# The last two heads' rows moved into the spare rows of the output projection's chunks, with a new written order for the last stages

## The chip, the cores and the metric

The kernel runs on one core of a Trainium2 chip. The metric is device microseconds of one execution, as the median of several. TensorE is called PE, VectorE DVE, ScalarE ACT, GpSimd POOL, and the engine that issues all DMAs here is SyncE, SP.

## The reference

One input x of 2048 rows and 640 columns goes through a linear attention with 32 heads of 20 and through a feed-forward layer of width 1728; a sigmoid gate g per row mixes the two.

```python
qkv = x @ wqkv                                    # 32 heads of 20
pq, pk = q @ w_phi, k @ w_phi                     # per head
phi = concat(softmax(p), softmax(-p))             # 40 features per head, of q and of k
kv, z = phi_k^T @ v, sum(phi_k)
o = (phi_q @ kv) / (phi_q @ z + 1e-6)
a = o @ wo
b = silu(x @ w1) @ w2
out = g * a + (1 - g) * b
```

## The kernel before

Everything is float32. Where accuracy matters PE multiplies in float32r, and each operand is split into a high and a low part, hi and lo; a product is then three passes, hi by hi, hi by lo, lo by hi. Splitting takes a copy on ACT (hi) and a subtraction on DVE or POOL (lo).

The rows of x are worked on as 16 tiles of 128, 8 blocks of 256 or 4 of 512. The first stages compute keys and values of all tiles and sum kv and z. Then the feed-forward layer runs, with the written orders HEAD and O1 to O10, in block products with fewer multiplications; its gated output goes to DRAM, as fb_d. The stage TAIL finishes the feed-forward layer, builds the query weights WQ (w_phi folded into wqkv, from loads of wqT) and does the queries of the last four tiles. The last stage, FIN, does the queries of the other twelve tiles, and for every block u the product with kv and the projection with wo.

An order is a string of names, and each name is a few instructions. The context manager `inorder` (L236) binds the instructions of PE, DVE, ACT and POOL to the order in which they are written, each engine for itself; SP isn't bound by it and is placed by the framework's scheduler. Before, each stage has its own `inorder`, so that instructions of two neighbouring stages can be interleaved.

The names of TAIL that matter here: fl is a load of 120 rows of wqT, fm the PE work that folds w_phi into them (L347), fs its split into WQ; hm and hp are the rest of the hidden tiles (L686) and their SiLU and split; im, ia and ig are output products, their addition and the gated store; km and kp make the weights kvw and kvwr from kv; ol and os load and split wo.

The names of FIN, with a query tile b of 0 to 11, a block u of 0 to 7, and p for a projection step:

- q0p and so on: the query projection, 30 matmuls (L596). q0m: maximum and minimum per head (L580, L581). q0s0, q0s1: the two differences (L587). q0e: the exp (L1335). q0S: sums (L1339). q0z: the product with z on POOL (L1352). q0Z: its sums (L1355). q0P, q0i, q0k: five small DVE steps (L1366 to L1382). q0M: scaling on POOL (L1388).
- t and f: t03 is PE's transposes of the features of block 0, group 3 (L1611), f03 the copy out of PSUM. Five groups hold six heads each, 120 features on either side; group 5 holds the last two heads, 80 features.
- n: the matmuls with kvw (L1727). The two sides of a group go to rows 0 to 63 and 64 to 127 of one bank. Each side has three heads, thus 60 rows; the four rows up to 64 are zero and unused.
- h and l: the split of n's result into oT, hi and lo (L1738, L1741 and L1747), for chunks 0 and 1, 2 and 3, and 4. A chunk is 128 rows of oT; there are five.
- w: the projection (L1780). Step p = 0, 1, 2 takes two blocks, 512 columns; steps 3 and 4 one block each, 256 columns. The digits after p are a part m0 of the output's five; in steps 3 and 4 the parts 0 and 2 do two at once. a and b are its two halves. d adds the feed-forward's part y, loaded from fb_d (L1772), and stores to out (L1791, L1792).
- x: x5l loads x columns for later queries (L321), x5s splits them.

The last two heads' 40 rows fit into no chunk. Before, kvwr is the 80 by 40 matrix three times side by side, so that n of group 5 gives 120 rows, three copies of the 40; `stk`, a small table of signs loaded from cst, turns them into hi, lo and hi (L1742, L1749), in the tile oR. wo's 40 rows are stacked in the same way in WOR (name R; L1286, L1287). One matmul of oR with WOR is then all three passes at once, the sixteenth term of a projection:

```python
TERMS = [(c, ho, hw) for ho, hw in PASSES for c in range(NG)] + [(NG, 0, 0)]
```

Of the kernel before, what the change touches and what calls it, by code (L numbers as in the profile page):

```python
# [8 lines left out]
F32 = mybir.dt.float32  # L9
F32R = mybir.dt.float32r  # L10
# [6 lines left out]
P = 128  # L17
S = 2048
D = 640
# [56 lines left out]
fl1 W fl5 fm1 fl2 fs1 fm0 ol1 fl3 hm012 fm2 fs0 fl4 fm3 fs2 fs3 wa hm013 hp012 fm5 fm4 fs4 hm113 fs5  # L76
km hp013 hm112 kp os1 qp12 hp113 q012 hp112 ol0 q112 qe12 wb qs12 im0 qn12 ia0 qN12 im1 qc12 qp13 ig0
q013 ia1 ol4 qP12 qi12 im2 q113 ol3 qe13 ia2 qw12 qs13 qm12 qc13 ol2 im3 qn13 ia3 ig1 qN13 qP13 os2
qp14 os0 qi13 q014 ig2 xl1 im4 q114 qw13 ig3 xl0 ia4 qm13 im5 os3 qe14 qs14 qn14 xs0 xs1 qc14 qp15
qN14 qP14 q015 ig4 xl2 ia5 im6 qi14 tm0 qw14 q115 tm1 qm14 os4 to0 qe15 qn15 ig5 qs15 ia6 ig6 qN15  # L80
to1 im7 ia7 qc15 im8 ia8 qP15 tm2 im9 qi15 ia9 xs2 tm3 ig7 qw15 qm15 ig8 ig9 to2 to3
# [62 lines left out]
t04 R t05 q0p q0m n000 n001 f04 f05 n010 h00 x5l n011 q0s0 h01 l00 l01 n020 n021 t10 h02 t11 f10 f11  # L144
l02 q0s1 t12 q1p t13 f12 x6l t14 q0e f13 q0z t15 q0S f14 q1m f15 q1s0 q1s1 q0Z n100 n101 h10 n110
n111 n120 x3s n121 h11 h12 q1e x4s x7l x8l x5s l10 l11 l12 x9l q0P q0i q1z q0k q0M q1S w00a w00b q1Z
w01a w01b q1P q1i d00 q1k q1M q2p q2m q2s0 q2s1 q2e d01 w02a w02b d02 q2z x6s x10l x7s x11l x8s x12l
t20 f20 t21 f21 t22 q3p q2S f22 t23 f23 q2Z t24 f24 t25 f25 q3m q3s0 q3s1 q3e q2P q2i q2k q3z q3S
n200 q2M n201 h20 n210 n211 h21 n220 n221 h22 w03a l20 q3Z w03b x9s q3P q3i l21 q3k l22 d03 q4p w04a
w04b q4m q4s0 q4s1 q4e q3M q5p q4z d04 q4S x13l x10s x11s x14l x15l t30 f30 q4Z t31 q4P f31 t32 f32  # L150
t33 q4i f33 t34 q5m f34 t35 f35 n300 q5s0 n301 q5s1 h30 n310 n311 h31 n320 n321 h32 q5e q4k q5z l30
q4M l31 l32 q5S w10a q5Z q5P w10b q5i q6p w11a w11b q5k q5M d10 q6m q6s0 d11 w12a w12b q6s1 q6e d12
q6z q6S x12s x16l x13s x14s x17l q7p t40 f40 t41 f41 t42 f42 t43 f43 q6Z t44 f44 q7m t45 f45 q7s0
q7s1 q7e q6P q6i q6k q7z q7S n400 n401 q6M h40 n410 n411 h41 n420 n421 h42 l40 q7Z q7P q7i q7k q7M
w13a w13b l41 l42 x15s d13 q8p w14a x16s x17s q8m q8s0 q8s1 q8e t50 f50 w14b d14 q8S q8z q9p q8Z t51
f51 t52 f52 t53 t54 f53 f54 t55 q9m q9s0 f55 q9s1 n500 n501 n510 h50 n511 h51 n520 n521 h52 q9e q8P
q8i q8k q9z l50 l51 q8M l52 q9S w20a w20b q9Z q9P q9i d20 q9k q9M q10p w21a w21b w22a q10m q10s0
q10s1 q10e d21 q10S w22b d22 q10z t60 f60 t61 f61 t62 q11p f62 t63 f63 q10Z t64 f64 t65 q11m f65
q11s0 q11s1 q11e q10P q10i q10k q11z n600 n601 h60 n610 n611 h61 q10M q11S n620 l60 q11Z n621 h62
q11P l61 q11i q11k l62 w23a q11M w23b d23 w24a w24b w30a d24 w30b d30 t70 f70 t71 f71 t72 f72 t73 f73  # L160
t74 f74 t75 f75 n700 n701 h70 n710 n711 h71 n720 n721 h72 l70 l71 l72 w32a w32b d32 w34a w34b d34
w40a w40b w42a d40 w42b d42 w44a w44b d44
# [8 lines left out]
def mix_kernel(ctx: ExitStack, tc: tile.TileContext, xT, wqT, wkc, wkr, wv, bd, bdc, cst, wo, w1, w1r, w2, out):  # L171
# [31 lines left out]
    def single(name):  # L203

        k = turns["single"] = turns.get("single", -1) + 1
        return ps.tile([P, 512], F32, tag=f"single{k % 4}", name=name, bufs=1)
# [29 lines left out]
    def inorder(*engines):  # L236
# [4 lines left out]
        prev = {}  # L241
# [16 lines left out]
    stk = cp.tile([P, 4], F32, name="stk")  # L258
# [16 lines left out]
    g_d = dp.tile([NT, P], F32, name="g_d")  # L275

# [49 lines left out]
    def xb_split(p, lo_eng="pool"):  # L326
        u, c = XP[p]
        r = xb.pop(p)
        t = slot(f"xb_{u}_{c}")
        split(t[:, 0, : r.shape[1]], t[:, 1, : r.shape[1]], r, lo_eng)  # L330
        if c == 0:
            X["t", u] = []
        X["t", u].extend(t[:, :, k * 256 : (k + 1) * 256] for k in range(r.shape[1] // 256))
# [233 lines left out]
    nc.sync.dma_start(stk, cst)  # L567
# [317 lines left out]
    with inorder(PE, ACT, DVE, POOL):  # L885
# [61 lines left out]
        with inorder(PE):  # L947
# [18 lines left out]
            nc.scalar.activation(warms, stk[:, :1], AF.Silu)  # L966
# [317 lines left out]
    def stack(dst, src, hi, col, n=GW):  # L1284

        nc.scalar.activation(hi, src, AF.Copy, scale=stk[:n, col : col + 1])  # L1286
        nc.vector.scalar_tensor_tensor(  # L1287
            dst, src, stk[:n, col + 1 : col + 2], hi.bitcast(F32), op0=ALU.mult, op1=ALU.add
        )

# [147 lines left out]
    def make_kvw():  # L1438

        nc.gpsimd.memset(kvw[:, :, KD:], 0.0)  # L1440
        pts = []
# [9 lines left out]
        for j0, n, pt in pts:  # L1451
# [165 lines left out]
    def t_out(u, i):  # L1617
# [280 lines left out]
```

## Time and profile before

| what | value |
|---|---|
| runs, us | 717.38, 716.41, 716.01; median 716.41 |
| profiled execution, span | 716.4 us; the page gives no other time of it |
| PE busy | 710.0 us, 99% |
| DVE, ACT, POOL busy | 471.9, 294.9, 389.4 us |
| DMA | 125.29 MB, mean 175 GB/s |
| TAIL | from about 480 to 545 us |
| FIN | from about 545 us to the end |

A row of a group is: line, engine, operation, out<-in by the program's names with shapes, count | busy us, mean ns of one | idle time of the engine before, with what ended it. PE's fp32 matmuls leave two records each. PE's durations overlap, since matmuls are pipelined; the pace is read from the chain of waits, whose rows are start, us, engine, what and count. PEld is the load of weights.

### The profile page before, as it was taken

The numbers are of one execution on the slowest core, as the hardware profiler recorded it, in microseconds if no ns is written. First come the engines' busy times: TensorE is split into PE (matmuls) and PEld (weight loads), VectorE is DVE, ScalarE is ACT, GpSimd is POOL, SyncE is SP. The second block draws the span as 40 slices with busy tenths as digits, with TensorE's granted clock in tenths as the row PEclk, the third lists the DMA queues.
The fourth block names the chain that finished last, engine by engine and source line by source line (L and its number), as shares of the span: only waits on it lengthen the run. The fifth ranks groups of instructions, "written<-read, shape, count | busy, mean of one in ns | idle before, by whom it ended". The sixth has DMA issues, their size and how long they took to land.

```text
span 716.4 us, 12133 instructions
## 1 busy us (share of the span) xinstructions
PE 710.0 (99%) x4671; PEld 604.7 (84%) x4671; DVE 471.9 (66%) x775; ACT 294.9 (41%) x557; POOL 389.4 (54%) x294
## 2 busy tenths in 40 slices
PE   9999999999999999999999999999999999999998
PEld 8888888888888888888888888788998888888887
DVE  4587988886353556679525556665888778687652
ACT  5444454556455233335344333435334343233240
POOL 2367876585743465132866547800599666574340
PEclk9999999999999999999999999999999999999999
DMA  8358878676775556195865633572033133111222
GB/s 312 130 184 301 311 267 325 247 279 230 217 245 192 178 200 228 52 339 189 290 232 199 213 108 121 191 235 59 17 109 118 49 126 96 65 63 45 89 81 67
DMA packets 52702, 125.29 MB, mean 175 GB/s; under 512 B 6896, under 2 KB 18564, under 8 KB 52644
## 3 DMA queue, kind: packets, MB, share of 16 engines
q1 hardware_dynamic: 52644, 124.51, 50.4%
q8 instruction: 37, 0.61, 0.3%
q14 instruction: 21, 0.17, 0.1%
HBM read 87.22 MB, written 37.27 MB: 174 GB/s over the span
## 4 chain that ended last, share of the span: by engine, by line
PE 97%; DMA 2%; SPq 0%; issue 0%; ACT 0%; DVE 0%
PE kvp L620 17%; PE o L1195 11%; PE o L1236 11%; PE pa L1780 11%; PE pq L596 10%; PE a L1106 9%; PE b L1106 3%; PE c L1106 3%; PE d L1106 3%; PE pn L1727 3%; PE o_m L1258 3%; PE ph L686 3%; PE pT L1611 3%; PE hp L705 2%; PE kvt L607 1%; PE kvp L490 1%
## 5 line engine op out<-in xcount | busy, mean ns | idle before, releaser
L1226 DVE TENSOR_TENSOR acc<-acc,o 128x512 f32<-128x512 f32 x104 | 68.3, 682 | 35.9 <-PE o L1236 35.8
L620 PE MATMUL kvp<-wh,xa 128*128 128x480 f32 (+2 forms) x420 | 90.4, 358 | 0.0
L1352 POOL TENSOR_TENSOR ez<-eq,zbc 128x1280 f32<-128x1280 f32 x16 | 48.5, 3030 | 74.8 <-ACT eq L1335 71.5
L1195 PE MATMUL o<-u,w 128*128 128x512 f32 x340 | 81.7, 391 | 0.0
L620 PEld LDWEIGHTS kvp<-wh,xa 128*128 128x128 f32 x420 | 72.8, 188 | 10.0 <-DVE ek L642 0.2
L1195 PEld LDWEIGHTS o<-u,w 128*128 128x128 f32 x340 | 63.4, 188 | 13.3 <-DVE acc L1200 0.3
L1780 PE MATMUL pa<-oT,wo 128*128 128x512 f32 (+1 forms) x375 | 74.1, 349 | 0.0
L1780 PEld LDWEIGHTS pa<-oT,wo 128*128 128x128 f32 x375 | 60.0, 188 | 11.3 <-issue 1.6
L1122 POOL TENSOR_TENSOR u<-v,u 128x512 fp32r<-128x512 f32 x16 | 20.7, 1296 | 64.1 <-ACT u L1121 64.1
L596 PE MATMUL pq<-wq,xb 128*128 128x320 f32 x360 | 55.1, 310 | 0.0
L648 POOL TENSOR_TENSOR ek<-ek,st 128x1280 f32<-128x1280 f32 x16 | 38.2, 2392 | 30.8 <-DVE st L647 13.2
L596 PEld LDWEIGHTS pq<-wq,xb 128*128 128x128 f32 x360 | 53.5, 188 | 1.0 <-ACT fT L1627 0.3
L1120 ACT ACTIVATE v<-v 128x512 f32<-128x512 f32 x33 | 20.9, 632 | 74.0 <-DVE v L1139 36.2
L1335 ACT ACTIVATE eq<-eq 128x1280 f32<-128x1280 f32 x16 | 20.4, 1277 | 71.3 <-DVE eq L587 70.0
L1090 POOL TENSOR_TENSOR v<-v,v 128x512 f32<-128x512 f32 x32 | 41.7, 1302 | 13.6 <-DVE u L1122 7.0
L620 PE MATMUL kvp<-wl,xa 128*128 128x480 f32 (+2 forms) x210 | 47.5, 355 | 0.0
L230 POOL TENSOR_TENSOR xa<-xra,xa 128x512 fp32r<-128x512 f32 (+1 forms) x26 | 28.4, 1115 | 23.9 <-ACT xa L228 23.9
L1388 POOL TENSOR_TENSOR eq<-eq,sm 128x1280 f32<-128x1280 f32 x16 | 37.9, 2371 | 5.4 <-DVE sm L1382 5.2
L620 PEld LDWEIGHTS kvp<-wl,xa 128*128 128x128 f32 x210 | 36.6, 188 | 4.7
L1627 ACT COPY fT<-pT 120x512 f32<-120x512 f32 (+1 forms) x48 | 23.1, 559 | 39.9 <-PE pT L1611 39.9
L1122 DVE TENSOR_TENSOR u<-v,u 128x512 fp32r<-128x512 f32 x25 | 19.9, 797 | 29.1 <-ACT u L1121 27.7
L1269 POOL TENSOR_TENSOR acc<-acc,G 128x512 f32<-128x512 f32 x20 | 27.6, 1401 | 13.6 <-DVE acc L1200 13.6
(247 smaller groups left out, 1586.5 us busy)
## 6 DMA issues: line engine op xcount, KB each, us to landing
w<-w_d SPq DMA_DIRECT2D x20, 640.0 KB
w_d<-aw SPq DMA_DIRECT2D x14, 640.0 KB
sa<-s_d SPq DMA_DIRECT2D x16, 512.0 KB
xr<-xT SPq DMA_DIRECT2D x27, 256.0 KB
ra<-w SPq DMA_DIRECT2D x18, 320.0 KB
wb<-w_d SPq DMA_DIRECT2D x9, 640.0 KB
w_k<-w SPq DMA_DIRECT2D x8, 640.0 KB
s_d<-as SPq DMA_DIRECT2D x10, 512.0 KB
```

The lines of the kernel that those rows point to most:

```text
L596: nc.tensor.matmul(dst, xt[c][:, hx, :], w[:, c, hw, lo : lo + n], start=first, stop=(hx == 1 and c == NC - 1))
L620: nc.tensor.matmul(kv_cols(t, lo, hi), xt[c][:, hx, :], WKV[hw][:, c, w_cols(lo, hi)], start=(n == 0), stop=(n == 3 * NC - 1), skip_group_ ...
L648: return lambda: nc.gpsimd.tensor_tensor(groups(e), groups(e), spread(st[:, 1, :]), op=ALU.mult)
L1090: nc.gpsimd.tensor_tensor(v[i], v[a], v[b], op=ALU.subtract)
L1106: last["mm"] = nc.tensor.matmul(out, lhs, rhs, start=(first and i == 0), stop=(stop and i == len(todo) - 1), skip_group_check=True)
L1122: eng.tensor_tensor(u[:, 1, :], v, u[:, 0, :].bitcast(F32), op=ALU.subtract)
L1195: nc.tensor.matmul(o, lhs, rhs, start=(n == 0), stop=(n == len(todo) - 1))
L1226: nc.vector.tensor_tensor(acc[j][m], acc[j][m], o, op=ALU.add)
L1236: nc.tensor.matmul(o, ws[hw], x()[hx], start=(first and i == 0), stop=(i == len(PASSES) - 1), skip_group_check=True)
L1352: nc.gpsimd.tensor_tensor(ez, Q[t]["e"], zbc, op=ALU.mult)
L1388: nc.gpsimd.tensor_tensor(groups(q["e"]), groups(q["e"]), spread(q["sm"][:, 2 * H : 4 * H]), op=ALU.mult)
L1780: nc.tensor.matmul(pa[:, a, :], wo_tile[0][:, c, hw, ds] if c < NG else WOR[:, ds], o[:, ho, c, :size] if c < NG else rest[:GW, :size], st ...
```

## The change

The four unused rows behind each side's 60 make eight per chunk, and 40 in five chunks: as many as the last two heads have. The change puts their rows there, and wo's rows likewise (by the host's layout of the input wo), so that a projection has 15 terms.

The rows have to cross partitions for that. kvwr holds its 40 columns once, padded to 64. z0m (r_mm) multiplies the 80 features of block 0's two tiles into the upper and lower half of 128 columns of the bank that t05 used, which is held until z0l. z0h and z0l split the result into a 128x128 pair rT; z0l also stores it to a DRAM tile r_d with two DMAs. z0d (r_place) reads it back with four DMAs into the spare rows of oT, behind h and l, which write all 128 rows. R, WOR, oR, cst and stk are gone. There are now n of a group by itself (n03) in place of n by pairs (n011).

TAIL and FIN are written in a new order, and the three stages' orders (HEAD to O10, TAIL, FIN) are one chain for each engine: nothing is pulled over a stage's end any more. The four single banks are one tag of four buffers, where the next tile takes any free one, in place of four tags in turn.

```diff
 TAIL = """
-fl1 W fl5 fm1 fl2 fs1 fm0 ol1 fl3 hm012 fm2 fs0 fl4 fm3 fs2 fs3 wa hm013 hp012 fm5 fm4 fs4 hm113 fs5
...
+fl5 fl4 fl1 xl2 hm012 ol2 fm1 fm5 fs1 fs5 W ol1 fm4 fm0 ol4 fl2 fl3 wa fs4 fs0 xs2 fm2 wb fm3 fs2 km
+hp012 fs3 qp12 q012 hm013 q112 qe12 qp14 ol3 hp013 q014 xl0 hm113 os1 qs12 qn12 xl1 q114 qe14 hp113
+qs14 qN12 os3 ol0 im0 hm112 qn14 qc12 qp13 q113 q013 hp112 ia0 im1 os2 qe13 qs13 qn13 qc14 xs0 qp15
+q015 ia1 im2 ia2 qc13 im3 qN13 ia3 im4 qP12 q115 ig1 ig3 os4 qN14 qi12 qe15 kp ia4 im5 ia5 im6 ig0
+qP13 qi13 ig4 qs15 xs1 os0 ia6 qw13 qm13 ig2 qn15 im7 ia7 im8 qw12 qm12 tm3 qc15 tm1 qP14 qN15 ig7
+qP15 qi14 qw14 qm14 ia8 im9 to1 qi15 qw15 to3 ia9 ig9 tm2 tm0 to2 qm15 ig8 ig6 ig5 to0
 """
 FIN = """
-t04 R t05 q0p q0m n000 n001 f04 f05 n010 h00 x5l n011 q0s0 h01 l00 l01 n020 n021 t10 h02 t11 f10 f11
...
+t05 f05 t04 q0p t15 f04 f15 x6l t11 t10 z1m f11 z0m f10 n00 z1h n02 z0h n01 n03 x4s q0m n04 z1l q0s0
+z0l x16l q0s1 h00 h02 h01 q0e q0z l00 x6s l02 n10 x3s n11 t12 x11l t13 l01 f12 t14 x5l x8l f13 q1p
+q0S z0d f14 n14 q0Z q0P q0i x7l h10 n12 x5s l10 q0k q1m n13 h12 l12 h11 l11 z1d x7s q0M q1s0 q1s1
+q2p w02a w02b q1e q1S x11s q2m w03a x10l q1z q1Z q1P q2s0 q1i x16s q1k d02 q1M q2s1 q2e q2z q2Z w01a
+q3p q3m q2S w00a q3s1 w01b q3s0 q3e x10s q2P w03b d01 w00b x14l t21 t22 q3z d03 x8s q2i q2k q3S t25
+f25 q4p t20 q3Z q2M x9l f21 q3P f22 f20 x15l d00 t23 f23 q3i q3k q3M t24 f24 x13l q4m q4s0 t35 z2m
+x12l n20 n21 f35 n24 z2h z3m n22 n23 t31 q4s1 z2l h20 l20 q4e q4S h22 h21 q5p q4z q4Z q4P q4i l22
+z3h x9s f31 w04a q5m z3l w04b l21 t30 f30 q5s0 t33 q5s1 q5e q5z t32 f32 q4k q5S t34 q6p f33 q5Z q4M
+f34 x14s x17l q5P q5i d04 q5k q5M n30 n34 x13s h32 n32 z2d n31 q6m l32 q6s0 h30 l30 n33 h31 t41 f41
+q6s1 q7p q6e x12s t43 f43 t44 f44 q6z l31 q6S q6Z q6P q7m q6i q6k t42 z3d t40 t45 f45 q7s1 f42 x15s
+q7s0 w12a f40 w12b d12 q7e q7z q7Z q7S w11a q8p w11b q7P q7i w10a w10b q8m n40 n41 q7k n44 d11 q6M
+z4m z4h d10 n42 n43 q7M t51 h40 q8s1 h42 q8s0 q9p q8e z4l l42 f51 h41 t52 f52 l40 q8S q8z q8Z q8P
+l41 t55 q9m t53 t54 t50 w14a w14b f53 q9s1 q9s0 f54 f55 q9e d14 n52 q9z x17s n53 f50 n50 z5m z5h n51
+h50 n54 h52 q11p h51 q10p w13a q8i z5l q8k q8M q9S q9Z q9P q9i q9k q9M q11m q11s1 q11s0 t61 l51 l50
+l52 t64 t63 q11e q11S z4d t62 w13b z5d w22a w21a q10m w21b q10s1 w22b w23a q10s0 f61 f62 q10e t60
+t65 w23b q11z q11Z f63 f64 q10z f65 f60 z6m q10Z n60 n61 n62 d13 n64 z6h h60 q10S h62 q11P q11i q10P
+n63 q11k d22 h61 d21 q11M q10i q10k q10M t73 t74 d23 f73 z6l l60 t71 t75 t70 f74 t72 f71 f75 w24a
+l62 w20a w24b w20b f70 n70 n71 l61 f72 n74 h70 h72 d24 n72 d20 n73 l72 z7m z7h z6d w34a l70 w34b z7l
+d34 w32a h71 l71 z7d w32b w30a w30b w42a d32 w40a w42b w40b d30 w44a d42 d40 w44b d44
 """
...
     def single(name):
-
-        k = turns["single"] = turns.get("single", -1) + 1
-        return ps.tile([P, 512], F32, tag=f"single{k % 4}", name=name, bufs=1)
+        return ps.tile([P, 512], F32, tag="single", name=name, bufs=4)
...
-    def inorder(*engines):
+    def inorder(*engines, prev=None):
...
-        prev = {}
+        prev = {} if prev is None else prev
...
-    stk = cp.tile([P, 4], F32, name="stk")
...
+    r_d = [dp.tile([2, REST, 256], F32, name=f"r_d{u}") for u in range(NP)]
...
-    nc.sync.dma_start(stk, cst)
...
+    chain = {}
+    with inorder(PE, ACT, DVE, POOL, prev=chain):
...
+        nc.gpsimd.memset(kvwr[:, REST:], 0.0)
...
         nc.scalar.copy(
-            kvwr.rearrange("p (k f) -> p k f", f=REST),
-            pt[:RC, None, n * KD : n * KD + REST].to_broadcast([RC, KH, REST]),
+            kvwr[:, :REST], pt[:RC, n * KD : n * KD + REST]
         )
...
-        kvwr = fs.tile([RC, P], F32, name="kvwr")[:, :GW]
+        kvwr = fs.tile([RC, CT], F32, name="kvwr")
...
-    WOR = tb.tile([GW, D], F32R, name="wor_s")
-    wor = raw("wor")
-    for k in range(3):
-        nc.sync.dma_start(wor[k * REST : (k + 1) * REST, :D], wo[NG * P :, :])
...
+    def r_mm(u):
+        f = fTs.pop((u, NG))
+        rests[u] = pr = rbank.pop(u)[:, 256:384]
+        for k in range(2):
+            nc.tensor.matmul(
+                pr[k * CT : (k + 1) * CT], kvwr, f[:RC, k * P : (k + 1) * P], start=True, stop=True, skip_group_check=True
             )
...
+    def r_hi(u):
+        t = tb.tile([P, 2, P], F32R, tag="rT", name=f"rT{u}", bufs=2)
+        nc.scalar.copy(t[:, 0], rests[u])
+        rests[u] = rests[u], t
+
+    def r_lo(u):
+        pr, t = rests.pop(u)
+        nc.vector.tensor_tensor(t[:, 1], pr, t[:, 0].bitcast(F32), op=ALU.subtract)
+        for k in range(2):
+            nc.sync.dma_start(
+                r_d[u][:, :, k * P : (k + 1) * P].rearrange("s r c -> r s c"), t[k * CT : k * CT + REST].bitcast(F32)
+            )
+
+    def r_place(u):
+        for side in range(2):
+            rows = slice(side * CT + KD, (side + 1) * CT)
+            for s in range(2):
+                nc.sync.dma_start(
+                    o_cols(u)[rows, s].bitcast(F32),
+                    r_d[u][s, side * REST // 2 : (side + 1) * REST // 2].rearrange("(c r) s -> r c s", r=CT - KD),
+                )
+
+    TERMS = [(c, ho, hw) for ho, hw in PASSES for c in range(NG)]
...
-    TERMS = [(c, ho, hw) for ho, hw in PASSES for c in range(NG)] + [(NG, 0, 0)]
...
-        half = len(todo) // 2
+        half = (len(todo) + 1) // 2
...
-                wo_tile[0][:, c, hw, ds] if c < NG else WOR[:, ds],
-                o[:, ho, c, :size] if c < NG else rest[:GW, :size],
+                wo_tile[0][:, c, hw, ds],
+                o[:, ho, c, :size],
...
+            for name, part in (("m", r_mm), ("h", r_hi), ("l", r_lo), ("d", r_place)):
+                ops[f"z{u}{name}"] = lambda u=u, part=part: part(u)
...
-        "cst": cst,
...
+                wo[: NG * GW].reshape(NG, 2, KD, D),
+                wo[NG * GW :].reshape(2, NG, CT - KD, D).transpose(1, 0, 2, 3),
```

126 lines of the change are left out of this document (41 added, 85 removed).

## The prediction

> **What bounds the kernel now.** I read the page first, then the chain of waits in order of time, then the waits of TensorE, then the groups of the last two stages with their shapes kept apart, and at last the SP queue's timeline.
>
> ```profile
> span 716.4 us, 12133 instructions
> PE 710.0 (99%) x4671; PEld 604.7 (84%) x4671; DVE 471.9 (66%) x775; ACT 294.9 (41%) x557; POOL 389.4 (54%) x294
> ...
> PEclk9999999999999999999999999999999999999999
> ...
> PE 97%; DMA 2%; SPq 0%; issue 0%; ACT 0%; DVE 0%
> ```
>
> TensorE is busy for 710.0 of 716.4 us, at a clock of nine tenths or more in every slice, and it is 97% of the chain. Time can come only from fewer or shorter matmuls, or from the 6.4 us in which PE is idle. The stretch of the final stage that the change touches most looks the same (columns: PE, PEld, DVE, ACT, POOL busy; clock, DMA share, GB/s):
>
> ```profile
> 600.00:630.00 30.00, 30.00 (x191) 26.64 (x190) 22.04 (x34) 9.84 (x19) 18.69 (x10) 1.00 0.26 83
> ```
>
> PE has no gap in 30 us; VectorE is at 73% and the DMA engines at 26%. So PE is the bound here, VectorE the next in line, and there is room in the DMA engines for some more bytes.
>
> **The change part by part.** *Matmuls taken out.* The chain (start, us, step, count) gives the pace of each kind, because PE's own durations overlap:
>
> ```profile
> 479.24 6.77 DMA wTq<-wqT
> ...
> 554.10 4.41 PE pq L596 x30
> ...
> 559.60 2.74 PE pn L1727 x24
> ...
> 617.35 7.37 PE pa L1780 x32
> ...
> 692.37 2.40 PE pT L1611 x22
> ...
> 697.52 15.30 PE pa L1780 x128
> ```
>
> 32 matmuls of 512 columns in 7.37 us are 0.230 each; 128 of 256 columns in 15.30 are 0.1195 each. The groups say how many of them are the sixteenth term, and how many multiply the last two heads:
>
> ```profile
> L1780 PE MATMUL pa<-oR,wor_s 120*128 120x512 f32 x15 | 6.0, 397 | 0.0
> L1727 PE MATMUL pn<-fT,kvwr 80*64 80x256 f32 x16 | 4.8, 379 | 0.0
> L1727 PE MATMUL pn<-fT,kvwr 80*56 80x256 f32 x16 | 4.8, 379 | 0.0
> L1780 PE MATMUL pa<-oR,wor_s 120*128 120x256 f32 x10 | 2.8, 282 | 0.0
> ```
>
> The sixteenth term goes: 15 x 0.230 = 3.45 us and 10 x 0.1195 = 1.20 us. The kvwr matmuls stay, but with 128 columns instead of 256, since the three stacked copies are no longer made: before, a block has four such records of the 24 that take 2.74 us, so 4 x 0.114 = 0.46 us. After, the two outputs still lie in different halves of the bank's rows, so I expect half, 0.23. The nearest row for 128 columns is the transposes, 2.40 / 22 = 0.109: four records that overlap in pairs would take 0.22, four in a row 0.44. The gain per block lies between 0.02 and 0.24 us; over eight blocks 0.2 to 1.9, and I take 1.8. No work is added to PE. Sum: 3.45 + 1.20 + 1.80 = 6.45 us, bounds 4.9 to 6.6.
>
> *Work beside PE.* Per block one VectorE step and one ScalarE step of the stack go, and a 128x128 pair for the rest comes; WOR's own stacking goes once, with its three loads.
>
> ```profile
> L580 DVE TENSOR_REDUCE mmq<-pq 128x32 f32<-128x640 f32 x12 | 9.8, 817 | 9.0 <-PE pq L596 9.0
> L581 DVE TENSOR_REDUCE mmq<-pq 128x32 f32<-128x640 f32 x12 | 9.7, 812 | 0.0
> L587 DVE TENSOR_TENSOR eq<-pq,mmq 128x640 f32<-128x640 f32 x12 | 9.8, 813 | 0.0
> L587 DVE TENSOR_TENSOR eq<-mmq,pq 128x640 f32<-128x640 f32 x12 | 9.7, 808 | 0.0
> L1335 ACT ACTIVATE eq<-eq 128x1280 f32<-128x1280 f32 x12 | 15.3, 1276 | 53.8 <-DVE eq L587 52.4 <-DVE sm L1366 1.3
> L1352 POOL TENSOR_TENSOR ez<-eq,zbc 128x1280 f32<-128x1280 f32 x12 | 35.6, 2966 | 47.5 <-ACT eq L1335 44.2 <-DVE sm L1382 3.2
> L1355 DVE TENSOR_REDUCE sm<-ez 128x64 f32<-128x1280 f32 x12 | 17.8, 1484 | 12.5 <-POOL ez L1352 12.5
> L1747 DVE TENSOR_TENSOR oT<-pn,oT 128x512 fp32r<-128x512 f32 x16 | 10.5, 677 | 3.5 <-ACT oT L1738 3.5
> L1749 DVE SCALAR_TENSOR_TENSOR oR<-pn,stk,oM 120x256 fp32r<-120x256 f32 x8 | 3.8, 474 | 0.0
> L1747 DVE TENSOR_TENSOR oT<-pn,oT 128x256 fp32r<-128x256 f32 x8 | 3.3, 416 | 0.4 <-ACT oM L1742 0.3
> L1791 DVE TENSOR_TENSOR y<-pa,y 128x256 f32<-128x256 f32 x2 | 0.9, 426 | 2.4 <-PE pa L1780 2.4
> L1287 DVE SCALAR_TENSOR_TENSOR wor_s<-wor,stk,wor_h 120x640 fp32r<-120x640 f32 x1 | 1.0, 1040 | 0.4 <-ACT wor_h L1286 0.4
> ```
>
> VectorE loses 8 x 0.474 + 1.04 = 4.8 us; a 128x128 subtraction, on the line through 0.677 at 512 columns and 0.416 at 256, takes an estimated 0.29, so 2.3 us come back. All this lies under PE work, worth nothing by itself; it only loosens the next engine. The same holds for the cst load, the smaller kvwr copy and the pool tags, which add no instruction to PE.
>
> *The start of the second to last stage.* Before, PE stood there for the wqT rows:
>
> ```profile
> PE pwq L347 <- DMA wTq<-wqT: 0.7, 1, 0.7
> ```
>
> ```profile
> 476.07 1.05 PE L347 MATMUL pwq<-constb,wTq 120*128 120x120 f32 x8
> ...
> 484.92 0.39 PE L686 MATMUL ph<-xf,w 128*128 128x512 f32 x1
> ...
> 486.06 2.49 PE L347 MATMUL pwq<-constb,wTq 120*128 120x120 f32 x20 [0.74 <-DMA wTq<-wqT]
> ```
>
> From 484.92 to 486.06 is 1.14 us, 0.91 over the 0.23 of a matmul's pace; the transfer issued at 479.24 landed 6.77 us later. In the new order all of fm1, fm5, fm4 and fm0 stand ahead of fm2, the first to need the late rows: some 5 us of other work (two fm take 2.49), so that even an equally late transfer is covered. I take off 0.9. The one chain forbids what the row at 476.07 shows, an fm pulled ahead into the stage before. That costs nothing: hm012 is the next instruction after Cm, and its operands come from loads of the earlier stages.
>
> *The trip through DRAM.* New on SP are two stores and four loads a block, 48 issues. A projection chunk's first matmul reads all 128 rows of a chunk, the spare ones too, so it waits for the four loads of both its blocks, and these wait for the last lo (l) of the block. Queued behind that wait stands all of PE. The trace has no such load; the nearest is a store of y whose buffer the next load takes over when it has landed. The five small VectorE steps (P, i, k) run from L1366 to the next reduction, 1.31 us:
>
> ```profile
> 564.79 0.18 DVE L1366 SCALAR_TENSOR_TENSOR sm<-pq,sm 128x32 f32<-128x32 f32 x1
> ...
> 566.10 1.48 DVE L1339 TENSOR_REDUCE pq<-eq 128x64 f32<-128x1280 f32 x1
> ```
>
> ```profile
> SPq L1772 <- DMA out<-y: 28.1, 15, 2.7
> ```
>
> ```profile
> 540.34 0.38 SPq L321 DMA_DIRECT2D xrb<-xT  x1
> ...
> 583.00 12.10 SPq L321 DMA_DIRECT2D xrb<-xT  x4
> ...
> 617.65 0.34 SPq L1792 DMA_DIRECT2D out<-y  x1
> 620.07 0.33 SPq L1772 DMA_DIRECT2D y<-fb_d  x1
> ```
>
> From issue to use is 2.42 us, and two issues of 0.34 stand ahead of the third load, which the first matmul needs: 3.1 us after the last l. Weighed chunk by chunk, from rows:
>
> Blocks 0 and 1 (w02a). From the end of q0p to w02a PE has 22 transposes (2.40), ten n (40 x 0.114 = 4.57), two z (0.46), q1p and q2p (8.82): 16.2 us. VectorE needs q0m, q0s0, q0s1 (3.25) and up to two z of 0.42; then come the exp (1.28) and ez (2.97), so q0Z starts at 7.5 to 8.3; then 1.48, the small steps 1.3, l10 0.68. q1m starts at 11.2 to 11.8 (q1p ends at 11.2), and 1.63 + 0.42 + 0.68 later l11 is done, at 13.9 to 14.5. Plus 3.1: the rows are there at 17.0 to 17.6, and PE has waited since 16.2. A wait of 0.8 to 1.4 us; I take 1.1, with 0 and 3.5 (one more landing) as bounds.
>
> Blocks 2 and 3 (w12a). From the end of q6p PE has five n (2.28), 22 transposes (2.40) and q7p (4.41): 9.1 us. VectorE has q6m, l32, q6s0, l30, q6s1, l31, 5.0 us, and up to 1 us left from before: 5.0 to 6.0, plus 3.1 is 8.1 to 9.1. Just covered; 0.2, bounds 0 and 2.
>
> Blocks 4 and 5 (w22a). From n54 on PE has two q (8.82), w13 (3.45) and four t (1.75), 14.0; VectorE is through l52 at some 9.5 (q11m waits for q11p, 4.4; then 1.63, 1.62 and 1.8 on top of what is left of q9), plus 3.1 is 12.6. Covered.
>
> Block 7 (w42a), the last: after w34b's end d34 (0.43) and l71 (0.68), plus 3.1, 4.2 us; w32 and w30 are 60 x 0.1195 = 7.2 us. Covered; if they were not, the end would move by the difference. The last add and store are those of before.
>
> For the waits of the new order that I have not walked I add 0.7, bounds 0 and 2.5.
>
> In a sentence by itself: the Trainium skill's page "DMA: Bandwidth & Descriptors", section "Anatomy of one DMA", gives some 2.0 us as the fixed cost of one DMA, most of it the receipt of the last write, measured on another issue path; by that figure the wait at w02a would be some 0.4 us shorter.
>
> Sum: 716.4 - 6.45 - 0.9 + 1.1 + 0.2 + 0.7 = 711.05, say 711.0. The span of the profiled execution is 716.4 us and the median of the runs 716.41, so nothing is to be converted.
>
> **The rivals.** *The rows come later than walked.* If VectorE is 1 us behind at each pair, the waits there are 2.1, 1.0 and 0 us; if it is 2 us behind, 3.1, 2.0 and 0.6. On top of 709.05 (716.4 - 6.45 - 0.9) and the 0.7, that is 712.9 to 715.4. For it: VectorE is at 73% and its order is strict. Against: it loses 2.5 us of work, and each wait lets it catch up.
>
> *Slower: the loads stand behind another transfer on SP.* The row at 583.00 shows four x loads that hold SP for 12.10 us, of which 4 x 0.38 is issuing: up to 10.6 us waiting for a raw slot, with nothing behind it let through. If one block's four loads are queued behind such an x load at w02a or w12a, PE waits up to 10.6 us instead of 1.1: 711.0 + 9.5 = 720.5. It decides from a wait of 6.5 us on (711.05 + 5.4 = 716.4), above which the change loses. Against: in this trace SP stood so only when no other transfer was due. The same page of the Trainium skill says that a semaphore wait happens on the issuing sequencer before dispatch; the trace agrees, with the 12.10 us.
>
> *No waits.* If the loads land earlier than the y row says and the order holds everywhere, the result is 709.05, with the largest saving 708.9.
>
> *It does not take out what it says.* If the z matmuls run one after the other (0.44) the gain is 1.6 us less, 712.6; this lies inside the range.
>
> **How the numbers follow.** The forecast gets 0.72; its own range is 709.7, with a third of the waits that I take (709.05 + 0.65), to 713.4, with the wait at w02a at its upper bound (711.0 + 2.4). Of the others, the later rows get 0.14, the blocked queue 0.07, no waits 0.07. A measurement of this kernel can tell 0.2%, 1.4 us, from no change: faster means under 715.0. Faster are the forecast, no waits and two thirds of the later rows, 0.88; the rest of those is within 0.2%, 0.05; the blocked queue is slower, 0.07. The range reaches from 708.8 to 714.2, which leaves out the blocked queue, half of the later rows and a little of no waits.
>
> **What would show it.** The pa groups should have 375 matmuls and none of oR; the last heads' matmuls should have 128 columns and come two by two; PE should no longer wait for wTq; the waits of PE should name a DMA at the first pa of a pair, longest at w02a. Wrong would be a PE wait of over 3 us at one place, PE work that falls by less than 5 us, or new idle time of PE in the second to last stage.

## The result, and the profile after

The changed kernel takes 735.89 us (median of 4 runs, 735.55 to 736.41), the kernel before in the same session 716.89 (716.01 to 717.84): a ratio of 1.0264, with an interval of 1.0249 to 1.0278. That is 19 us slower; the prediction was 711.0 and its range ended at 714.2. The profiled execution took 735.78 us, its span is 733.9.

The page of the changed kernel, in the lines that answer to those of before:

```profile
span 733.9 us, 12149 instructions
...
PE 710.3 (97%) x4646; PEld 601.9 (82%) x4646; DVE 469.5 (64%) x774; ACT 298.8 (41%) x560; POOL 387.8 (53%) x295
...
PE   9999999999999999999999999999979789899998
...
PE 77%; DVE 7%; POOL 6%; issue 5%; ACT 3%; DMA 2%; SPq 0%; POOLq 0%; DVEq 0%; ACTq 0%
```

PE has 25 matmuls fewer and is as long "busy" as before (710.0). It is no longer alone on the chain: 97% has become 77%, and VectorE, GpSimd and "issue" (time in which an engine waited for nothing that the profile shows) have most of the rest. The slices show where: the first 29 of the 40 are full, and then PE has gaps in nearly every slice.

The groups of matmuls show that the work did go (columns: line, operation, shape, count, busy, mean ns, idle before):

```profile
L1782 PE MATMUL pa<-oT,wo 128*128 128x512 f32 x225 | 53.8, 394 | 1.7 <-DMA oT<-r_d 1.7
L1782 PE MATMUL pa<-oT,wo 128*128 128x256 f32 x150 | 17.9, 280 | 0.0
L1729 PE MATMUL pT<-fT,kvwr 80*64 80x128 f32 x32 | 3.1, 282 | 0.0
```

375 pa matmuls and none of oR; the 32 narrow ones come in pairs, four in 0.22 to 0.32 us, 2.1 us for eight blocks. Before, by the prediction's average over the 24 matmuls of n, they took 8 x 0.46, so that about 6.2 us of work are gone, against 6.45 predicted. The trace of before has a better figure, from their first start to the next step's:

```profile
561.74 0.61 PE L1727 MATMUL pn<-fT,kvwr 80*64 80x256 f32 x4
562.27 3.73 PE L1780 MATMUL pa<-oT,wo 128*128 128x512 f32 x15
```

That is 0.53 a block, and 6.8 us of work gone in all. What came instead shows in the stretches of the last two stages (PE, PEld, DVE, ACT, POOL; clock):

```profile
520.00:545.00 25.00, 20.18 (x94) 16.44 (x92) 20.37 (x28) 7.38 (x16) 21.79 (x17) 1.00 0.33 108
545.00:570.00 25.00, 24.23 (x168) 20.48 (x168) 13.35 (x26) 11.50 (x24) 19.61 (x19) 0.93 0.25 78
570.00:600.00 30.00, 25.02 (x133) 21.20 (x133) 19.63 (x31) 7.75 (x13) 15.87 (x10) 1.00 0.23 70
600.00:630.00 30.00, 27.43 (x185) 23.55 (x184) 20.80 (x37) 11.36 (x23) 18.43 (x10) 0.94 0.23 70
```

Two things are new: in two of these stretches PE idles 5 us of 25 or 30, and in the other two its clock falls to 0.93 and 0.94. The waits of PE name the causes (total, times, longest):

```profile
PE pT L1599 <- POOL eq L1377: 6.7, 2, 4.5
PE pq L592 <- DVE sm L1371: 2.9, 3, 2.1
PE pq L592 <- POOL xb L228: 2.1, 1, 2.1
PE pa L1782 <- DMA oT<-r_d: 1.7, 1, 1.7
PE pT L1599 <- DVE y L1793: 1.6, 3, 0.8
PE pn L1705 <- DVE y L1793: 1.2, 1, 1.2
```

In the trace of before, PE's longest wait from the first products on was the 0.7 us for wqT. Only 1.7 us of the new waits is the trip through DRAM. The rest is GpSimd (the scaling of the query features that the transposes read, and a split of x) and VectorE (the step that frees a pair bank, one of the two pairs of banks that the query projections write; the add that frees a single bank). The answer for the line that frees a pair bank tells it most directly; its last lines list who waited for it. In the changed kernel:

```profile
L1371 DVE SCALAR_TENSOR_TENSOR sm<-pq,g,sm x12: 272/281/284, 568.8 to 697.0; 128x64 f32<-128x64 f32 x12
...
  POOL eq L1377: 13.0, 6
  PEld pq L592: 4.7, 5
  PE pq L592: 2.9, 3
```

and the same step in the kernel before:

```profile
L1382 DVE SCALAR_TENSOR_TENSOR sm<-pq,g,sm x12: 271/284/287, 565.9 to 687.8; 128x64 f32<-128x64 f32 x12
...
  POOL eq L1388: 5.2, 5
  POOL ez L1352: 3.2, 1
```

Before, this step was late for GpSimd, and PE never felt it. After, PE stands behind it.

To count it all, take for each step of the written order the time from its first matmul to the next step's first, less its matmuls times the paces of the prediction's rows. These extras sum to 3.4 us in the second to last stage and 3.5 in the last before, and to 9.4 and 20.4 after: 22.9 us more. With 6.2 us of work less that makes 716.4 - 6.2 + 22.9 = 733.1, beside a span of 733.9. (With 0.53 for 0.46 both terms grow by 0.6 and the sum stays.)

The largest single place, on PE:

```profile
545.38 1.45 PE L1599 MATMUL pT<-ident,eq 128*120 128x128 f32 x8 [4.52 <-POOL eq L1377]
546.49 4.12 PE L1191 MATMUL o<-u,w 128*128 128x512 f32 x11
```

and on GpSimd, in the same stretch:

```profile
521.93 2.97 POOL L1341 TENSOR_TENSOR ez<-eq,zbc 128x1280 f32<-128x1280 f32 x1 [10.28 <-ACT eq L1324]
...
539.13 2.92 POOL L1341 TENSOR_TENSOR ez<-eq,zbc 128x1280 f32<-128x1280 f32 x1
542.01 0.88 POOL L1369 TENSOR_TENSOR sm<-sm 128x64 f32<-128x64 f32 x1
542.97 2.36 POOL L1377 TENSOR_TENSOR eq<-eq,sm 128x1280 f32<-128x1280 f32 x1
```

tm3, the transposes at 545.38, needs the feature tile that GpSimd finishes at 545.3. GpSimd had stood idle 10.28 us for an exp, and was then busy, but for two gaps of 0.5 us, to beyond tm3. And after the wait the 11 matmuls need 4.0 us, where their pace makes 2.5. The clock (last but two) says why:

```profile
540.90:545.40 4.50, 0.02 (x1) 0.02 (x1) 4.42 (x4) 0.00 (x0) 4.42 (x4) 1.00 0.19 58
...
547.00:549.00 2.00, 2.00 (x6) 1.55 (x5) 0.70 (x3) 0.95 (x2) 1.84 (x5) 0.50 0.35 131
```

There are two such stretches at half clock, from 546.0 and from 604.0, of some 3.4 us each. So an estimated 3.4 us (2 x 3.4 x 0.5) of the 22.9 are not waits but PE at half its pace behind them.

### The profile page after: what moved, and what is told of

It is laid out like the page before. It is cut to its first block, busy times and chain, and to the rows that moved or that the text cites. A ratio compares the mean times of both kernels' runs of the same rounds, so it can differ in the third digit from the quotient of the medians.

```text
span 733.9 us, 12149 instructions
## 1 busy us (share of the span) xinstructions
PE 710.3 (97%) x4646; PEld 601.9 (82%) x4646; DVE 469.5 (64%) x774; ACT 298.8 (41%) x560; POOL 387.8 (53%) x295
## 4 chain that ended last, share of the span: by engine, by line
PE 77%; DVE 7%; POOL 6%; issue 5%; ACT 3%; DMA 2%; SPq 0%; POOLq 0%; DVEq 0%; ACTq 0%
PE kvp L616 17%; PE o L1232 11%; PE a L1102 9%; PE o L1191 8%; PE pa L1782 4%; POOL ez L1341 3%; PE b L1102 3%; PE c L1102 3%; PE d L1102 3%; PE o_m L1254 3%; PE pq L592 2%; PE ph L682 2%; PE hp L701 2%; POOL eq L1377 2%; PE kvt L603 1%
## 5 line engine op out<-in xcount | busy, mean ns | idle before, releaser
L1782 PE MATMUL pa<-oT,wo 128*128 128x512 f32 (+1 forms) x375 | 71.7, 349 | 1.7 <-DMA oT<-r_d 1.7
L592 PE MATMUL pq<-wq,xb 128*128 128x320 f32 x360 | 57.5, 318 | 5.0 <-DVE sm L1371 2.9
L228 POOL TENSOR_TENSOR xb<-xrb,xb 128x512 fp32r<-128x512 f32 (+1 forms) x18 | 19.9, 1106 | 42.0 <-PE pwq L344 23.8
L1344 DVE TENSOR_REDUCE sm<-ez 128x64 f32<-128x1280 f32 x16 | 23.7, 1483 | 26.3 <-POOL ez L1341 26.3
L1324 ACT ACTIVATE eq<-eq 128x1280 f32<-128x1280 f32 x16 | 20.4, 1276 | 49.2 <-DVE eq L583 40.1
```

Of the source, the lines that this page charges most:

```text
L228: eng.tensor_tensor(lo, src, hi.bitcast(F32), op=ALU.subtract)
L592: nc.tensor.matmul(dst, xt[c][:, hx, :], w[:, c, hw, lo : lo + n], start=first, stop=(hx == 1 and c == NC - 1))
L1782: nc.tensor.matmul(pa[:, a, :], wo_tile[0][:, c, hw, ds], o[:, ho, c, :size], start=(i == 0), stop=(i == len(TERMS) - 1),)
```

## The experiments

The first theory was **order**: the rows are harmless, and the newly written orders cost the time. The rival **trip** put it down to the way through DRAM, wherever it stands in the order; a third was **chain**. The common tag of the four single banks stayed in every run made from the changed kernel and was not run by itself; PE's waits that name a step freeing a single bank sum to 3.4 us in the changed kernel (1.6, 1.2 and 0.6). All ratios are to the kernel before on the same chip.

**e1 to e4: the rows with the orders of before.** In e1 both orders are those of before, with the narrow product where the stacked one stood and three query projections put ahead of a pair's first sum, to cover the trip; e2 is e1 without the one chain; e3 and e4 put back one order each.

```diff
 TAIL = """
-fl5 fl4 fl1 xl2 hm012 ol2 fm1 fm5 fs1 fs5 W ol1 fm4 fm0 ol4 fl2 fl3 wa fs4 fs0 xs2 fm2 wb fm3 fs2 km
...
+fl1 W fl5 fm1 fl2 fs1 fm0 ol1 fl3 hm012 fm2 fs0 fl4 fm3 fs2 fs3 wa hm013 hp012 fm5 fm4 fs4 hm113 fs5
...
 FIN = """
-t05 f05 t04 q0p t15 f04 f15 x6l t11 t10 z1m f11 z0m f10 n00 z1h n02 z0h n01 n03 x4s q0m n04 z1l q0s0
...
+t04 t05 q0p q0m n00 n01 f04 f05 n02 h00 x5l n03 q0s0 h01 l00 l01 n04 z0m t10 h02 z0h t11 f10 f11 l02
...
```

> The changed kernel with the written orders of before in its last two stages: the names of the rows (z) stand where the stacked product and its split stood, the stacking of WOR is gone, and one query projection is put ahead of the first projection chunk of each of the first three pairs, so that the trip through DRAM has cover. One chain as in the change. Theory 'order' (the new written orders bring the waits, the rows take out 6.3 us of PE work): 709.5 to 712 us. Rival 'rows' (the trip through DRAM, its 48 issues on SP and the bank that is held longer bring the waits): 722 us or more, with PE waits on oT<-r_d of several us. Rival 'chain' (forbidding the stages to overlap costs most): 716 or more, with the loss at the start of the second to last stage.

> The kernel of e1 without the chain: each stage is in order for itself, as before. Theory 'order': within 1 us of e1, since the chain forbids only one fm pulled ahead. Rival 'chain': 5 us or more below e1.

> The changed kernel with the order of before in the second to last stage alone; the last stage keeps the new one. Theory 'order': the waits beside PE's work grew by 6.2 us in that stage and by 16.8 in the last; with the old order in the second to last 6 to 7 us come back: a span of 727 to 728. Rival 'rows': no change in the last stage, and the second to last has no rows, so the same 6 us, but then e4 stays above 725. If the late start of the last stage is itself what gives that stage its waits, 720 or less.

> The changed kernel with the last stage's order of e1; the second to last keeps the new one. Theory 'order': 16 to 17 us come back, a span of 717 to 718, with all that is left in the second to last stage. Rival 'rows': above 725.

With the chain: both orders old (e1) 749.22 us (ratio 1.0441, 1.0416 to 1.0466), old tail and new end (e3) 734.76 (1.0247, 1.0230 to 1.0264), new tail and old end (e4) 750.03 (1.0452, 1.0428 to 1.0476), both new 735.89. So with the chain the new order of the last stage is worth 14 us to the rows, that of the stage before nothing: in e3 PE waits 4.25 us in that stage at a fused product, where the chain costs the kernel before its time too (e8 below). The old order of that stage was not run with the new end and no chain. Without the chain (e2) 740.78 (1.0335, 1.0315 to 1.0356). The theory 'order' in its first form fell: the old orders are worse, 'rows' had e1 and e4, and 'chain' the 8.4 us between e1 and e2; e3 came out above every range named for it. In e2 PE waits

```profile
PE pa L1781 <- DVE oT L1720: 7.6, 3, 3.0
PE pq L592 <- DVE sm L1371: 4.8, 3, 4.0
PE pa L1781 <- DMA oT<-r_d: 3.9, 2, 2.7
```

for VectorE's low parts and for banks, and of these three least for the trip.

**e5, e10, e6: the rows early in each block, in the old orders, without and with the loads.**

```diff
     def r_place(u):
-        for side in range(2):
...
+        pass
...
```

> The rows with the orders of before, each stage for itself, as in e2, but no query projection is moved, the last group is transposed first, its z matmul and split stand ahead of the other n, so that their bank comes free early, and the four loads back from DRAM are left out: the last two heads are missing from the output. It asks what the 15 terms are worth when nothing has to wait for the rows. Theory 'trip' (the wait for the rows, from n to the first projection matmul, is what costs, directly or through the work that had to be moved to cover it): 717.0 - 6.3 = 710.7 us, 710 to 712. Rival 'banks' (z and its bank cost as much): 714 or more.

> e5's kernel once more, for a profile (old orders, no chain, last heads' transposes and product early in each block, the four loads back left out, so the last two heads are missing). Its time was 720 to 722.6 and not the 710.7 of the work alone. Theory 'banks': the bank that the early transpose holds until the low half is subtracted, and its later neighbours, show as PE waits at the transposes and at n of each block, over 6 us in sum, all named after VectorE or ScalarE steps of the same block. Rival 'loads and x': the waits name POOL or DMA. Rival 'pace': no PE waits beyond those of before, but matmuls at a longer pace.

> e5 with the four loads. Every first projection matmul now waits for the rows, and nothing is moved to cover it. Theory 'trip': per pair the last l some 2 us behind n, then 3.1 us, so 4 to 5 us three times and up to 3 us for the two last blocks, 13 to 18 us above e5, with the clock's loss 725 to 730. Rival: less than 5 us above e5, then it was the moves in e1 and e2 and not the trip.

e5: 722.08 us (1.0058, 1.0039 to 1.0078); one of its four runs, the profiled one, took 1419.74 us with PE busy for 1413.4, about twice as long for the same work, and is left out of the ratio; its cause is not known. e10, the same kernel run once for a profile: 721.12. With the loads, e6: 748.24 (1.0438, 1.0389 to 1.0487). So the uncovered trips cost 26 us, where 13 to 18 were expected. But even without them the kernel is 11 us above what its work makes (717.03 - 6.2 = 710.8). e10's waits say where most of that sits, at the projection and not at the transposes and n, where they were expected:

```profile
PE pa L1775 <- DVE rT L1739: 7.4, 5, 2.3
```

There is no load here, so the sum needs nothing of rT; what joins them in the program is the bank of the block's last transposes, now held until VectorE has subtracted the low part, while n takes the other three of the four. 'Trip' is right about e6, though not about the size, and 'banks' about e5.

**e7: the changed kernel without the loads** (edit as in e5; the last two heads are missing).

> The changed kernel without the four loads back (the last two heads are missing). Theory 'order' (in the changed kernel the trip is covered, and the cover itself brings the waits): only the one wait on oT<-r_d goes, 1.7 to 1.9 us, 733.5 to 734.5. Theory 'trip alone': 10 us or more come back, below 726.

736.65 us (1.0268, 1.0253 to 1.0283): no gain, not even the 1.7 us of w02a, which 'order' had expected back. The wait at w02a is gone, but q3p waits that much longer for its bank, 4.1 us where it was 2.1:

```profile
PE pq L592 <- DVE sm L1371: 4.5, 2, 4.1
```

VectorE frees that bank at the same time in both (PE goes on at 585.1 and 585.2), and it sets the pace there. In the changed kernel the trip is covered; the cover is what costs.

**e8, e13: the chain alone.** e8 gives the kernel before one chain; e13 takes it from the changed one (the edit shown, at each of the three stages).

```diff
-    with inorder(PE, DVE, ACT, POOL, prev=chain):
+    with inorder(PE, DVE, ACT, POOL):
...
```

> The kernel before with one chain for its three stages and nothing else. Theory 'chain': with the old orders, e1 lay 8.4 us above e2 (6.0 in the profiled spans), so 5 to 8 us above before, 722 to 725, with the wait at the second to last stage's fm1 and fm0. Rival: within 1 us of before, as the prediction priced it, if that loss needs the rows too.

> The changed kernel without the one chain: each of the last three stages is chained by itself, so that an engine may run ahead over a stage's border as before; orders as changed. Theory 'chain': as in the kernel before (e8, +6.4 us), the chain costs several us here too: 728 to 731. Theory 'order': the new order of the second to last stage has put hm012 and others ahead of the fused products, PE's waits there are few, and the waits at 540 and after come from GpSimd and the banks, within the stages: 734.5 to 736.5, change under 1.5 us.

e8: 723.41 us (1.0083, 1.0066 to 1.0100), 6.4 more, as 'chain' had it. e13: 741.25 (1.0336, 1.0322 to 1.0350), 5.4 more than with the chain; neither theory had the sign. In e8 the fused products that PE had begun a stage early come after the border, and the second of them (fm0) waits:

```profile
484.47 2.49 PE L347 MATMUL pwq<-constb,wTq 120*128 120x120 f32 x10 [4.25 <-DVE wq L230]
```

In e13 it is hm012 that moves ahead into the stage before, and the fused products come in pieces and wait:

```profile
485.03 0.41 PE L344 MATMUL pwq<-constb,wTq 40*128 40x40 f32 x2 [0.74 <-DVE wq L228]
486.51 6.30 PE L344 MATMUL pwq<-constb,wTq 120*128 120x120 f32 x40 [1.07 <-DVE acc L1222]
```

They end 3.4 us later than in the changed kernel (492.8 against 489.4). One chain is neither good nor bad; it fixes an order that one list was written for and the other was not.

**e9: the sixteenth term by itself**, left out of the kernel before (the last two heads are missing).

```diff
-    TERMS = [(c, ho, hw) for ho, hw in PASSES for c in range(NG)] + [(NG, 0, 0)]
+    TERMS = [(c, ho, hw) for ho, hw in PASSES for c in range(NG)]
```

> The kernel before, with the sixteenth term of each output sum left out (so the last two heads are missing from the output); everything else, orders and stack included, as before. It prices the term by itself. Theory 'work': TensorE is the bound, so 15 x 0.230 + 10 x 0.1195 = 4.65 us come off whole: 712.4 (711.5 to 713.3), PE's waits as before. Rival 'pace': PE's time is set by what feeds it (banks, VectorE), and less than half of it comes off: above 714.7.

712.12 us (0.9934, 0.9919 to 0.9949), 4.55 below before, 4.65 expected. The term is worth its matmuls, whole. From e9 to e7, both without rows to wait for, are some 24 us (on two chips): the new orders, the chain, the early product and the common tag.

**e11: no table loads.** In the second to last stage Exp and Silu now alternate on ScalarE, with five table loads instead of one. e11 uses Exp for the three late hidden tiles (another function, for its time only).

```diff
-            nc.scalar.activation(ph, ph, AF.Silu)
+            nc.scalar.activation(ph, ph, AF.Exp if h and j else AF.Silu)
...
```

> The changed kernel, with Exp in place of Silu in the three hidden tiles of the second to last stage that come after the first exp of a query tile (their part of the output is thus another function). No table is then loaded again: 1 load in that stage instead of 5. Theory 'table loads': the 4 loads of 1.28 us sit ahead of the exps that GpSimd waits for; its queue is then 3 to 5 us earlier, the wait of 4.7 us at 540 shrinks by as much, and the time falls to 731 to 733. Theory 'VectorE and GpSimd order': the exps wait for VectorE's eq anyway, and the time falls by less than 1.5 us: 734.4 to 736.

735.56 us (1.0262, 1.0246 to 1.0277): nothing, as 'VectorE and GpSimd order' had it. The exps waited for VectorE anyway: one came 2.0 us sooner (518.57 against 520.58) and GpSimd's tile 1.6 us sooner, yet PE's wait for that tile stayed 4.5 us.

**e14, e15, e17: half of GpSimd's scaling, half of VectorE's sums, both** (10 of the 20 columns of each group, so the output is another).

```diff
-        nc.gpsimd.tensor_tensor(groups(q["e"]), groups(q["e"]), spread(q["sm"][:, 2 * H : 4 * H]), op=ALU.mult)
+        n = slice(0, DH // 2)
+        e, m = groups(q["e"])[:, :, n], spread(q["sm"][:, 2 * H : 4 * H])[:, :, n]
+        nc.gpsimd.tensor_tensor(e, e, m, op=ALU.mult)
...
-        nc.vector.tensor_reduce(sums[t], groups(Q[t]["e"]), axis=AX.X, op=ALU.add)
+        nc.vector.tensor_reduce(sums[t], groups(Q[t]["e"])[:, :, : DH // 2], axis=AX.X, op=ALU.add)
...
```

> The changed kernel with GpSimd's multiplication of the query features by their weights done on half of the columns (10 of the 20 in each group; the other half stays unscaled, so the output is another). GpSimd gets some 1.2 us per tile back, on 16 tiles. Theory 'GpSimd': the waits of PE at the transposes (4.5 us at 540, 2.4 at t41), at q4p (x split on GpSimd, 2.1) and the half clock behind them shrink by more than half: 728 to 731. Theory 'banks and VectorE': these waits pass on to the next releaser, and the time falls by less than 3 us: above 733.

> The changed kernel with both of VectorE's sums over a query tile (1.5 us each) taken over half of each group (the output is another). VectorE gets up to 0.75 us per sum back, 32 sums. Theory 'banks and VectorE': the pair banks come free 1.5 us earlier per tile (the waits of 2.1 and 2.3 us at q2p and q3p go), y and l steps are on time, and GpSimd's multiplications start earlier too: 725 to 730. Theory 'GpSimd': only the waits that name VectorE shrink: 731 to 734.

> The changed kernel with e14's and e15's edits together: GpSimd's multiplication and both VectorE sums of a query tile over half of each group (the output is another). Theory 'the two engines' lateness': the gains add up or more (4.6 + 7.7): 723.5 or below, and PE's waits at the transposes and pair banks go. Rival 'they share waits': each wait has both engines in its chain, so that the gains overlap: 725 to 728.

e14: 731.25 us (1.0207, 1.0190 to 1.0223), 4.6 off, between the two theories and nearer to 'GpSimd'; PE's waits for the scaling fall from 6.7 to 3.5 us, the one for the x split stays at 2.1. e15: 728.20 (1.0156, 1.0136 to 1.0177), 7.7 off, within the range of 'banks and VectorE', but not by the waits that it named: one of 2.1 us at a pair bank stays, as do 6.5 us for GpSimd's scaling; what went are smaller waits for VectorE (1.6, 1.2, 0.9, 0.7 and 0.6 us). e17: 722.35 (1.0077, 1.0060 to 1.0095), 13.5 off, a little more than the sum, as 'the two engines' lateness' had it. By the count of extras e17 has 3.2 us left in the second to last stage, as before the change, and 11.9 in the last. Its longest waits:

```profile
PE pT L1601 <- POOL eq L1379: 2.7, 2, 2.0
PE pq L592 <- POOL xb L228: 2.1, 1, 2.1
PE pa L1784 <- DMA oT<-r_d: 1.4, 1, 1.4
```

The extras have fallen from 29.8 to 15.1 us, toward the 6.9 of before: most of the new waits hang on steps of these two engines. Their work is what it was (VectorE 469.5 us against 471.9, GpSimd 387.8 against 389.4), and in the order of before PE waited for none of these steps. The rest (x split, trip, banks) was not taken apart further, and no order was run that keeps all the rows and gives these steps their slack back.

**e12, e16, e18: a version that gains.** The kernel before, its orders and 16 terms, with the rows only for the blocks of 256 columns: both in e12, block 7 alone in e16 and e18, where w30 and w32 stand behind block 7's last subtraction, and w34 ahead of t70 (for which l61 moves ahead of q11Z). e16 also moves hm013 ahead of fm2, which waited for wqT.

```diff
-... w24a w24b w30a d24 w30b d30 t70 ...
+... w24a w24b w34a d24 w34b d34 t70 ...
...
-... l72 w32a w32b d32 w34a w34b d34 w40a ...
+... l72 w30a w30b d30 w32a w32b d32 w40a ...
```

> The kernel before, with the rows only for the last two blocks (u = 6 and 7, the outputs of 256 columns): their last heads' product with 128 columns in the bank it had, stored and loaded back into the spare rows as in the change, 15 terms in their ten half-width sums; the other six blocks keep the stack and 16 terms; orders unchanged, no chain. Saved: 10 x 0.1195 = 1.2 us and 2 x 0.24 = 0.5 us. Theory 'cover': the trip of some 3.1 us after the last l lies under w23 and w24 (14 us) for block 6 and w32 and w34 (5.4 us) for block 7, PE waits nowhere, and the time is 1.7 us below before, ratio 0.9976 (0.997 to 0.9985). Rival 'trip costs anyway' (loads late, output loads queued behind them): no gain or a loss, ratio 1.000 or above.

> The kernel before with the rows for block 7 alone, with a cover that needs no projection pulled ahead: w30 and w32 (64 matmuls of 0.1195, 7.6 us) stand between the last l of block 7 and w40, w34 goes ahead of t70; trip 5.1 to 5.8 us after the last l, as e12 showed, not 3.1. Also hm013 stands ahead of fm2, which waited 0.9 us for wqT. 16 terms elsewhere, no chain. Saved: 5 x 0.1195 = 0.6, 0.24, and 0.9 us. Theory 'cover': 1.7 us below before, ratio 0.9976 (0.996 to 0.999). Rival 'nothing is free': the w34 moved ahead waits for a bank or the trip is longer than its cover: ratio 1.000 or above.

> The kernel before with the rows for block 7 alone, as e16 but with the second to last stage as in before (hm013 not moved). In e16 the stretch from the first matmul of w23 to PE's end took 31.05 us against 31.86 in before, PE waited nowhere in it, and the move of hm013 only exchanged a wait of 0.9 us for one of 1.1. Theory 'cover': 0.8 us below before, ratio 0.9989 (0.998 to 0.9998). Rival 'nothing is free': 1.000 or above.

e12: 725.41 us (1.0116, 1.0099 to 1.0133), 8.7 slower, with 1.7 us of work less; the rival had it. VectorE's last low part of block 6 stands behind the sums and small steps of the last query tile, while PE is already in w23 and w24:

```profile
687.50 0.28 DVE L1766 TENSOR_TENSOR oR<-pn,oR 128x128 fp32r<-128x128 f32 x1
```

then SP stores and loads (start, time):

```profile
687.85 0.70 SPq L1768 DMA_DIRECT2D r_d<-oR  x2
...
689.79 1.33 SPq L1774 DMA_DIRECT2D oT<-r_d  x4
```

and PE goes on at 693.60, after 6.5 us of waiting and then at half clock:

```profile
693.60 6.13 PEld L1812 LDWEIGHTS pa<-oT,wo 128*128 128x128 f32 x30 [6.50 <-issue]
```

The whole trip is 693.60 - 687.78 = 5.8 us. e16: 716.81 (1.0001, 0.9992 to 1.0009): in the last stage PE waits nowhere, but the moved hm013 makes it wait 1.1 us for VectorE where wqT had cost it 0.9; the rival had it. e18: 715.94 (0.9985, 0.9976 to 0.9994): 1.3 us below before, within 'cover', where five terms and one narrow product make 0.8. It is a small gain, but its interval ends below 1. Its end on PE is one row without a wait,

```profile
702.94 9.00 PE L1812 MATMUL pa<-oT,wo 128*128 128x256 f32 x75
```

the loads having been issued from 698.62 on.

## Why the prediction was wrong, point by point

*Matmuls taken out* (6.45 us): right. 4.55 by e9, and 1.6 for the narrow products by the prediction's price of before, or 2.2 by the starts in the trace, where 1.8 was taken.

*The scale* ("nothing is to be converted"). Wherever a run has both, its time is 1.7 to 2.1 us above its span (735.78 and 733.9 here), so a span of 716.4 goes with a time of some 718.2. That it equalled the median was chance. This is small beside the miss.

*Work beside PE* (VectorE 2.5 us less): 471.9 has become 469.5. "Worth nothing by itself": right.

*The start of the second to last stage* (-0.9, and the chain "costs nothing"): the wait for wqT is gone, and the fused products run without a gap. About the chain the argument was too short: e8 and e13 price it at +6.4 in the old orders and -5.4 in the new ones. In the changed kernel it is no loss, so "costs nothing" held there, but not for the reason given.

*The trip.* w02a waited 1.7 us, 1.1 predicted; w12a, w22a and w42a are covered as walked. But the 3.1 us after the last l were too few. At w02a VectorE's last l ends at 571.50,

```profile
570.49 1.01 DVE L1721 TENSOR_TENSOR oT<-pn,oT 128x256 fp32r<-128x256 f32 x2
```

SP issues the four loads at once,

```profile
571.53 1.30 SPq L1750 DMA_DIRECT2D oT<-r_d  x4
```

and PE's first sum starts 4.2 us after that l, though the stores were long done:

```profile
575.73 7.36 PE L1782 MATMUL pa<-oT,wo 128*128 128x512 f32 x31 [1.71 <-DMA oT<-r_d]
```

Where the store too comes after the last l, as in e12, it is 5.8. The prediction had one more landing as its upper bound; the 1.7 us here lie 0.6 above its value. (By its own prices q1p ends at 10.5 us, not 11.2, since only seven n stand ahead of it; VectorE was later, so this moved nothing.)

*The step that failed* is "For the waits of the new order that I have not walked I add 0.7, bounds 0 and 2.5." They are some 22 us: 22.9, plus the 0.9 that went at the start of the second to last stage, less the 1.7 at w02a. About 3.4 of them are the half clock behind two waits, for which the sum had no term. In e17, where only steps of GpSimd and VectorE are shorter, 14.7 of them are gone (29.8 - 15.1). The prediction's own walk to w02a held the warning: PE reaches q2p at 16.2 - 4.4 = 11.8 us after q0p, and VectorE frees q2p's bank (q0k) at 8.3 + 1.5 + 1.3 + 0.7 = 11.8 at the latest. That is no slack at all, and it was walked for the rows and not for the bank. Measured, PE is there at 12.2 and the bank comes free at 12.5. The next ones (q3p 2.1 us, q4p 2.5, the transposes behind GpSimd 4.5 and 2.2) were not walked, because in the trace of before PE stood in none of them. That trace showed waits that did not happen in the old order, not how near they were.

*The rivals.* The blocked SP queue had the sign right and the mechanism wrong: without any loads (e7) the time is the same. The rows being late is what the new order avoids, but for the 1.7 us at w02a; left uncovered it costs far more than that rival had (e6). Of the three signs named as "wrong", two came: a wait over 3 us at one place (4.5), and new idle time in the second to last stage. The third, PE work down by less than 5 us, did not.

## What to carry to other kernels

A matmul taken out of a kernel bound by TensorE is worth its whole pace if nothing else in the order changes (e9). If its removal puts a latency on the path, the cover has to be pulled ahead from somewhere: for each step pulled ahead, walk when its bank comes free and when its operand is made, on VectorE and GpSimd as well, before it is called cover. That PE never waited for an engine at 65% with a strict order doesn't show that this engine has slack at the step that matters.

## What the runs showed of the hardware

A wait of PE can cost more than its length. In e8, after 4.25 us without a matmul, the granted clock was 0.50 from 484.4 on, and still

```profile
488.50:491.00 2.50, 2.50 (x8) 1.97 (x7) 0.00 (x0) 0.00 (x0) 0.00 (x0) 0.53 0.00 0
```

that is over 6 us at about half pace; in e12, after 6.5 us, it was 0.50 up to 699. In the changed kernel the wait of 2.10 us in q4p was followed by half clock, and the one of 2.19 us at t41 was not:

```profile
604.20:606.00 1.80, 1.80 (x8) 1.80 (x8) 1.66 (x7) 0.00 (x0) 1.63 (x1) 0.50 0.47 149
...
631.00:634.00 3.00, 1.63 (x12) 1.64 (x13) 3.00 (x6) 0.89 (x2) 2.55 (x2) 1.00 0.30 105
```

The Trainium skill's page "TensorE: Matmul & The Clock Gate", section "What's actually happening", has the clock halve after an idle window of some 3.4 us, and come back after a busy one; the windows run freely and are not reset by the kernel. The waits of 4.25, 4.5 and 6.5 us agree; the 2.10 us in q4p, with shorter waits just ahead of it, do not fit a single idle window of that length, and what decides there is open.

A table load on ScalarE took 1.28 us, and the next instruction followed at once:

```profile
497.96 0.58 ACT L669 COPY ur<-ph 64x512 f32<-64x512 f32 x1
498.56 1.28 ACT L671 ACT_TABLE_LOAD   x1
499.85 0.63 ACT L671 ACTIVATE ur<-ur 64x512 f32<-64x512 f32 x1
```

Four of them more cost this kernel nothing measurable (e11).
